# A two-layer attention and FFN kernel: the order of all engines, planned at build time before, written out as a table after

## The chip, the core and the metric

The kernel runs on one core of a Trainium2 chip. The metric is the device time of one launch in microseconds (us), median of several runs. The engines are PE (TensorE, matrix products; its weight loads are shown apart, as PEld), DVE (VectorE), ACT (ScalarE), POOL (GpSimd) and SP (SyncE, which here only issues DMAs). Each engine works through its own queue in the order in which the program lists it, and waits on semaphores where an operand comes from another engine.

## The reference, cut to what matters

x is 2,048 rows of 512 values in bf16, cut into 4 segments of 512 rows. Two layers follow each other, each of them attention and then an FFN, both on normalised rows and both added to x.

```python
x = A_x
x = x + _A_ref(_layernorm(x), wq, wk, wv, wo, beta)
x = x + _B_ref(_layernorm(x), w_gate, w_up, w_down)
x = x + _A_ref(_layernorm(x), wq, wk, wv, wo, beta)   # the same weights again
x = x + _B_ref(_layernorm(x), w_gate, w_up, w_down)

# _A_ref, for segments s = 0..3, with 32 heads of 16 values
p = softmax(qs @ ks.T * scale + causal_mask)          # inside the segment
a_mem = (phi(qs) @ M) / (phi(qs) @ z + 1e-06)         # phi(t) = t + 1 if t > 0 else exp(t)
o = g * a_mem + (1 - g) * (p @ vs)                    # g = sigmoid(beta), one per head
M = M + phi(ks).T @ vs ; z = z + phi(ks).sum()        # memory for the later segments
# _B_ref, with 1,792 hidden values
return (gelu(x @ w_gate) * (x @ w_up)) @ w_down
```

## The kernel before, in words

**Pieces of work.** The work is 8 pairs of an attention part and an FFN part, k = 0 to 7: layer k // 4, segment k % 4. An FFN part needs its own attention part, and an attention part of the second layer needs the FFN part of the same segment in the first. So the FFN of one segment can run beside the attention of the next ones, and nearly all of the span does so.

**Attention part k** (class `Att`, L799). Normalised rows `xn` (L734) are turned to `xnT`, by a DMA issued on SP (L577) or by PE with an identity matrix (L425). PE makes q, k and v by dense products of 128 x 512 (four of them, one per 128 rows of the weight, add up in one PSUM bank). The results are copied out of PSUM by DVE (L601) or ACT (L602), whichever the planner picks. `kx` is a masked copy of k (L546, L551). The scores are made in 72 rounds of 256 columns, two rounds to a visit (`score`, L1670): each visit is a run of small products with row tiles (32 or 16 rows, four tiles side by side) into four PSUM banks. ACT exponentiates two banks at a time, 1,024 values per row, or all four at once, 2,048 (L1710), into `pt`; POOL or DVE masks it (L1646, L1651, L1656). Value products (a "flush", `flush_item`, L1165) multiply `pt` with the values (`vaug`, `vz`, and `gel_sb` for k = 0) in column tiles: 128 rows by 32 columns, four side by side. DVE turns and scales the result (`byq` L1209, `ab` L1225, `aT` L1232). The memory part has small products (`mblk`, `zcols`, `phik`), with phi made by ACT (`e`, L966), a clipping on DVE or POOL (L989) and a sum on DVE (L970).

**FFN part k** (class `Ffn`, L1278). It adds the attention's output to x (L1287), takes the moments (L684), normalises, and makes 14 gate products (`wg_sb`), a gelu on ACT (L1448, L1323, L1337), 14 up products (`wu_sb`) that DVE multiplies in (L1388), and four down products of 14 steps each (`wd_sb`), added to x by DVE (L1287) and written out by SP.

**Three ways of tiling PE.** Whole (128 x 128), row tiles (scores) and column tiles (values). A dense product can be made whole, or as four column tiles of 32 columns each: the same result, four weight loads and four matmuls in place of one each. `product` (L605) decides:

```python
if ck.mode == "columns" or ck.mode == "rows" and (any(it.kind == "flush" and it.near() for it in items)):
    ck.tiling("columns")
    for c in range(4):
        r = slice(32 * c, 32 * c + 32)
        multiply(out[r], lhsT=lhsT[:, r], rhs=rhs, start=start, stop=stop, tile_position=(0, 32 * c))
else:
    ck.tiling("whole")
    multiply(out, lhsT=lhsT, rhs=rhs, start=start, stop=stop)
```

So once column tiles are in use they stay until the next score visit.

**What sets the order.** `order` (L402) plays the kernel through while it is built. It holds a clock (`Clocks`) with a duration for each operation, a model of each engine's queue, of PSUM banks that come free (`pick`, L1626), of slots and DMAs, and some 130 numbers (`POLICY`, `CHANGES` by 20 us, `NUDGES`, `VISITS`) that say how urgent each kind of work is. Step by step it takes the next score visit, value product or dense product that its clock calls ready, and writes the instructions of all engines as its clock serves them. A dense product that has begun is mostly run to its end (unless a part of its input is still missing). Where its clock finds no work for PE it writes a dummy product of 128 columns on a tile of ones (`warm`), so that PE goes on:

```python
if streams:
    ps = Psum()
    ps.bank = bank
    product(ps()[:, 0:P], warm[:], wide[:, 0, :])
```

All of this happens at build time: the chip gets a fixed order for each engine. All matmuls are issued in a helper, so that they have line 421 in the profile, and transposes by PE line 425.

Of the kernel before, what the change touches and what calls it, by code (L numbers as in the profile page):

```python
# [48 lines left out]


def shared(*tiles):
    return [(b, BOTH, ki, P * ki, C, C * n) for n, (b, ki) in enumerate(tiles)]


def whole_block(b):
    rounds = []
    for par in range(2):
        rounds += [([(b, (par,), *piece) for piece in pieces], n) for pieces, n in zip(FULL, DIAG)]
        if not par:
            rounds.append((shared(*((b, ki) for ki in range(TPS))), None))  # L60
    return rounds, ((0, 0, SHARED + 1), (1, SHARED, ROUNDS))


def table(halved):

    rounds, units = [], []

    def add(got):
        rounds.extend(got)
        return range(len(rounds) - len(got), len(rounds))  # L70

    def early(b):
        return [([(b, (par,), *piece) for piece in EARLY], 2) for par in range(2)]

    def late(b):
        return [([(b, (par,), *piece) for piece in pieces], n) for pieces, n in LATE for par in range(2)]

    for b in range(1 if halved else KT):
        got, parts = whole_block(b)
        at = add(got)  # L80
        units.append((b, None, [((par,), [at[i] for i in range(i0, i1)]) for par, i0, i1 in parts]))
    if halved:
        a1, s12, a2 = add(early(1)), add([(shared((1, 0), (1, 1), (2, 0), (2, 1)), None)]), add(early(2))
        a3, s3 = add(early(3)), add([(shared(*((3, ki) for ki in range(TPS))), None)])
        units += [(1, 0, [(BOTH, [*a1, *s12])]), (2, 0, [(BOTH, [*a2, *s12])]), (3, 0, [(BOTH, [*a3, *s3])])]
        units.append((3, 1, [(BOTH, [*s3, *add(late(3))])]))
        l1 = add(late(1))
        s12 = add([(shared((1, 2), (1, 3), (2, 2), (2, 3)), None)])
        units += [(1, 1, [(BOTH, [*l1, *s12])]), (2, 1, [(BOTH, [*s12, *add(late(2))])])]
    assert len(rounds) == STEPS  # L90
    flushes = [(u, b, h, n, pars, used) for u, (b, h, fl) in enumerate(units) for n, (pars, used) in enumerate(fl)]
    return rounds, len(units), flushes


TABLES = [table(k in HALVED) for k in range(NK)]
FLUSHES = [[[f for f in TABLES[k][2] if max(f[5]) == t] for t in range(STEPS)] for k in range(NK)]
USERS = [[sum(t in f[5] for f in TABLES[k][2]) for t in range(STEPS)] for k in range(NK)]
UNIT0 = [sum(TABLES[i][1] for i in range(k)) for k in range(NK)]
FLUSH0 = [sum(len(TABLES[i][2]) for i in range(k)) for k in range(NK)]


BY_PE = {("xnTf", 0), ("xnTf", 1), ("xnTf", NK - 1)}
QUICK = {("xnTf", k): (2,) for k in HALVED}
# [11 lines left out]
POLICY = dict(
    flush_wait=-12.009, piece_slack=-25.599, kb_slack=-71.296, mem_slack=-20.591, qk_due=-62.012, e_q=-288.808,
    e_k=138.109, exp_slack=-4.686, e_slack=148.266, phi_slack=52.68, gelu_slack=19.624, act_evict=2.071,
    first_evict=4.769, gate_step=1.835, up_due=3.98, up_step=-6.05, down_due=84.578, down_step=14.696, upd_due=9.144,  # L120
    kb_act=663.078, vz_slack=0.687, x_dve=-0.049, v0_due=-232.366, x1_at=-21.812, x2_at=-35.702, x3_at=1.468,
    x3_load=-242.902, direct=2, gelu_tiles=0, look=-61.488, lag=0, wv_at=-9.865, xn_pool=-26.108, kb_pool=62.128,
    cut_pool=0.028, at_pool=-27.695, gate_due=4.711, shun=77.466, col_gap=6.814, hold=34, early=435.185,
    starve=-5.581, near=-26.359, cap=6, soon=-134.054, drain=-0.14, join=0, held=10, urge_a1=-29.527, urge_a2=-0.64,
    urge_a3=-0.468, urge_a4=-5.519, urge_a5=-268.031, urge_a6=-6.935, urge_a7=-34.222, urge_f0=-37.767,
    urge_f1=-6.779, urge_f2=-11.706, urge_f3=-0.081, urge_f4=51.11, urge_f5=-14.712, urge_f6=-5.12, urge_f7=-38.117,
    half_a1=14, half_a4=21, half_a5=4, half_a6=18, half_a7=14, half_f0=21, half_f1=8, half_f2=10, half_f3=24,
    half_f4=46, half_f5=6, half_f6=8, pair_a1=10, pair_a2=3, pair_a3=12, pair_a4=11, pair_a5=0, pair_a6=65,
    pair_a7=28, pair_f0=9, pair_f1=19, pair_f2=43, pair_f3=2, pair_f4=22, pair_f5=23, pair_f6=28, pair_f7=11,
    turn_a1=14, turn_a2=12, turn_a3=8, turn_a4=8, turn_a5=6, turn_a6=16, turn_a7=42, turn_f2=18, turn_f3=4,  # L130
    turn_f4=16, turn_f5=2, turn_f6=6)

# [1723 lines left out]
```

## Time and profile before

| what | before |
|---|---|
| median of 3 runs (lowest, highest) | 539.28 us (539.02, 539.95) |
| the profiled execution, its span | 539.06 us (the page gives 539.1) |
| instructions | 20,839 |
| matmul records, weight loads on PE | 9,006, 9,072 |
| HBM read, written | 9.70 MB, 2.10 MB |
| granted PE clock, all 40 slices | 9 (90% or more) |

The profiled execution is one run of the same program, 0.2 us under the median; one core, so that its span is its time. The page gives busy time of each engine and its share of the span. A row of a group reads: line, engine, operation, out<-in, shapes, count | busy time and mean duration in ns | idle time of the engine just before, and what ended it. A row of the timeline reads: start and length in us, engine, line, operation, count, and in brackets the idle time before. A matmul's recorded end is modelled, and consecutive matmuls overlap in the records, so that durations of single matmuls add up to more than PE's time; the distance of their starts is what PE needs. A row of waits reads: who waited for whom, us in total, times, longest.

### The profile page before, as it was taken

To read this page: it belongs to the slowest core of one execution; us is meant where nothing else is said; L and a number is where in the kernel's file an instruction comes from. 1 tells how busy PE (TensorE), PEld (TensorE's weight loads), DVE (VectorE), ACT (ScalarE), POOL (GpSimd) and SP (SyncE) were. 2 spreads that over 40 slices of the span, in tenths; PEclk is the share of its full clock that TensorE was granted. 3 is DMA by queue.
4 is the path that set the end of the run, shared out by engine and by line. 5 is a ranking of instruction groups with operands and counts; after the bars stand their busy time and mean duration, and the time that the engine had idled before them with its cause. 6 is when DMAs were issued, how large, how long until landed. Compare 5 with 4: busy or idle time off the path is not lost.

```text
span 539.1 us, 20839 instructions
## 1 busy us (share of the span) xinstructions
PE 521.3 (97%) x9006; PEld 274.5 (51%) x9072; DVE 449.0 (83%) x849; ACT 433.2 (80%) x559; POOL 286.2 (53%) x360
## 2 busy tenths in 40 slices
PE   8999999999999999999999999999989999999997
PEld 4444467446654454554544454454554456555444
DVE  7998897899999997898997999878988786786342
ACT  6999997998999978999899778889789968830320
POOL 4997853279778656647572387550655253301000
PEclk9999999999999999999999999999999999999999
DMA  8349302422011123311432120310121004100001
GB/s 270 85 109 208 93 19 54 128 41 62 13 32 41 24 46 49 52 33 21 52 80 32 23 43 12 71 35 9 33 71 24 0 16 98 14 2 30 11 0 40
DMA packets 69134, 27.96 MB, mean 52 GB/s; under 512 B 53426, under 2 KB 69042, under 8 KB 69042
## 3 DMA queue, kind: packets, MB, share of 16 engines
q1 hardware_dynamic: 68752, 26.36, 22.1%
q8 instruction: 71, 1.16, 0.9%
q10 hardware_dynamic: 290, 0.26, 0.1%
q14 instruction: 21, 0.17, 0.1%
HBM read 9.70 MB, written 2.10 MB: 22 GB/s over the span
## 4 chain that ended last, share of the span: by engine, by line
PE 77%; DVE 11%; DMA 4%; issue 3%; POOL 3%; ACT 2%; DVEq 0%; POOLq 0%; ACTq 0%
PE ps L421 76%; DVE st L684 2%; DVE x_sb L1287 2%; ACT pt L1710 2%; DVE xn L734 2%; DMA xnT<-xn 2%; DMA amT<-am 2%; DVE byq L1209 1%; DVE ab L1225 1%; POOL pt L1646 1%; PE ps L425 1%; DVE phiq L970 1%; POOL rs L721 0%; DMA x_sb<-in_A_x_dram 0%; POOL pt L1651 0%
## 5 line engine op out<-in xcount | busy, mean ns | idle before, releaser
L1710 ACT ACTIVATE pt<-ps 128x1024 bf16<-128x1024 f32 (+1 forms) x274 | 277.8, 1072 | 39.5 <-PE ps L421 34.4
L1646 POOL TENSOR_SCALAR_AFFINE_SELECT pt<-pt 128x256 bf16<-128x256 bf16 (+1 forms) x192 | 108.2, 577 | 143.1 <-ACT pt L1710 138.3
L421 PE MATMUL ps<-xnT,wg_sb 128*32 128x512 bf16 (+3 forms) x940 | 106.5, 362 | 1.4 <-issue 1.1
L421 PE MATMUL ps<-wd_sb,gel_sb 128*32 128x512 bf16 (+3 forms) x879 | 102.8, 364 | 2.9 <-issue 1.9
L421 PE MATMUL ps<-xnT,wu_sb 128*32 128x512 bf16 (+1 forms) x816 | 99.6, 379 | 0.6 <-issue 0.2
L1388 DVE TENSOR_TENSOR gel_sb<-gel_sb,ps 128x512 bf16<-128x512 bf16 x112 | 74.4, 682 | 23.6 <-PE ps L421 22.1
L421 PEld LDWEIGHTS <-gel_sb 128*32 128x32 bf16 (+1 forms) x1086 | 50.7, 97 | 45.1 <-issue 4.8
L421 PEld LDWEIGHTS <-wu_sb 128*32 128x32 bf16 (+1 forms) x826 | 44.4, 97 | 50.2 <-issue 0.6
L421 PEld LDWEIGHTS <-wg_sb 128*32 128x32 bf16 (+1 forms) x954 | 46.9, 97 | 38.3 <-issue 2.0
L1287 DVE TENSOR_TENSOR x_sb<-x_sb,ps 128x512 bf16<-128x512 bf16 (+1 forms) x68 | 43.1, 642 | 20.5 <-PE ps L421 20.2
L1209 DVE STREAM_TRANSPOSE byq<-ps 128x512 f32<-128x512 f32 x64 | 45.2, 709 | 14.6 <-PE ps L421 13.4
L989 POOL TENSOR_SCALAR e<-e 128x512 bf16<-128x512 bf16 x31 | 49.8, 1608 | 3.8 <-ACT e L966 3.1
L1651 POOL TENSOR_SCALAR_AFFINE_SELECT pt<-pt 64x1024 bf16<-64x1024 bf16 x34 | 39.4, 1158 | 14.7 <-ACT pt L1710 10.0
L1448 ACT ACTIVATE gel_sb<-gel_sb 128x512 bf16<-128x512 bf16 (+1 forms) x81 | 45.9, 652 | 0.1
L684 DVE BATCH_NORM_STATS2 st<-x_sb 128x6 f32<-128x512 bf16 x60 | 40.8, 679 | 0.3
L601 DVE CAST gel_sb<-ps 128x512 bf16<-128x512 f32 x48 | 32.3, 680 | 7.9 <-PE ps L421 7.4
L421 PE MATMUL ps<-pt,vaug 128*32 128x256 bf16 (+2 forms) x1344 | 35.4, 239 | 0.2 <-POOL pt L1646 0.2
L421 PE MATMUL ps<-xnT,wk_sb 128*32 128x512 bf16 (+3 forms) x238 | 33.8, 353 | 0.5 <-issue 0.3
L421 PE MATMUL ps<-xnT,wq_sb 128*128 128x512 bf16 (+3 forms) x205 | 32.3, 347 | 2.0 <-DMA xnT<-xn 0.9
L421 PEld LDWEIGHTS <-vaug 128*32 128x32 bf16 x1344 | 26.7, 97 | 11.6 <-issue 4.2
L421 PE MATMUL ps<-q,kx 32*128 32x64 bf16 (+2 forms) x1120 | 30.8, 217 | 0.8 <-DVE x_sb L1287 0.8
L421 PE MATMUL ps<-wv_sb,xnT 128*32 128x512 bf16 (+1 forms) x194 | 30.6, 380 | 1.1 <-issue 0.6
(116 smaller groups left out, 704.4 us busy)
## 6 DMA issues: line engine op xcount, KB each, us to landing
vz<-vaug SPq DMA_DIRECT2D x14, 136.0 KB, 2.9
wg_sb<-in_B_w_gate_dram SPq DMA_DIRECT2D x8, 224.0 KB, 4.0
wu_sb<-in_B_w_up_dram SPq DMA_DIRECT2D x8, 224.0 KB, 4.4
wd_sb<-in_B_w_down_dram SPq DMA_DIRECT2D x7, 256.0 KB, 3.5
x_sb<-in_A_x_dram SPq DMA_DIRECT2D x3, 512.0 KB, 6.6
out_dram<-x_sb SPq DMA_DIRECT2D x12, 128.0 KB, 1.8
xnT<-xn SPq DMA_TRANSPOSE x48, 2.4
wk_sb<-in_A_wk_dram SPq DMA_DIRECT2D x2, 256.0 KB, 4.2
```

The costliest lines, as they stand in the source:

```text
L421: nc.tensor.matmul(*args, **named)
L601: ck.dve.post(ck.made(), slack + pol.drain, (0.673, lambda: nc.vector.tensor_copy(out=dst(), in_=src()), end), taken=taken)
L684: nc.vector.bn_stats(out=self.st6[:, 0, :], in_=x_sb[:, self.tt0 + j, :])
L734: eng.tensor_scalar(out=xn[:], in0=x_sb[:, self.tt0 + j, :], scalar1=self.mv[:, j, 1:2] if self.quick else self.mv[:, j, 0:1], scalar2=sel ...
L989: lambda eng: eng.tensor_scalar(out=e[0][:], in0=e[0][:], scalar1=1.0, scalar2=None, op0=ALU.min), summed)
L1209: nc.vector.transpose(out=(self.byq[:, pars[0], :, :].rearrange("p a c -> p (a c)") if h is None else self.byq[:].rearrange("p u a c -> p ...
L1287: ck.dve.post(ck.made(), slack, (0.15 + 0.00104 * (c1 - c0), lambda: nc.vector.tensor_tensor(out=xt, in0=xt, in1=ps()[:, 0:c1 - c0], op=AL ...
L1388: ck.dve.post(ck.made(), pol.drain, (0.683, lambda: nc.vector.tensor_tensor(out=g, in0=g, in1=ps()[:], op=ALU.mult), lambda t: (ps.read(t) ...
L1448: return (0.205 + 0.427 * (f1 - f0), lambda: nc.scalar.activation(out=g, in_=g, func=ACT.Gelu_apprx_tanh), lambda t: self.gelu_done(t, f0, ...
L1646: nc.gpsimd.affine_select(out=view, in_=view, pattern=[[0, 4], [0, n], [1, C]], compare_op=ALU.is_ge, fill=0.0, base=C, channel_multiplier=-1)
L1651: nc.gpsimd.affine_select(out=view, in_=view, pattern=[[0, 4 * TPS], [1, C]], compare_op=ALU.is_ge, fill=0.0, base=0, channel_multiplier=-1)
L1710: nc.scalar.activation(out=pt_all[:, slots[0]:slots[0] + 2, 2 * p:2 * p + 2 * n, :].rearrange("p r h c -> p h r c"), in_=ps_all[:, b0:b0 + ...
```

## The change

The planner goes. In its place stands a table, `ORDER`, of 2,559 entries, in which each entry is one step of one engine: its code, then its numbers. `Q/1/0/0/4/0/1` is four steps of the q product of part 1, block 0, into bank 0, as column tiles (last number 1); `S/0/0/4/6/0` is a score visit of part 0 into the banks from 4 and from 6 and slot 0; `e` and `E` are exponentials of two and of four banks; `F` is a value product; `W`, `G`, `P`, `O` are down, gate, up and output products; `l` and `L` are gelus; `M` masks; `Zu`, `Zg`, `Zo`, `Zd` load weights, `X` a segment of x. `run` reads the entries and calls a function for each. The bank, the tiling, the engine and the place are thus given per entry, and a dense product may be cut into pieces of 1, 2 or 3 steps with other work between them. The table has no dummy products. The operations themselves are the same, down to their shapes; only the start of the program (to the first score visit) has its old order.

Counted in the two built programs, before and after: 9,072 and 10,757 matmuls on PE. Dense products of 512 columns: 1,235 and 786 whole, 1,924 and 3,720 instructions of column form (four to a product). Changes of tiling on PE: 319 before, 365 after. Exponentials of two banks: 260 to 146, of four banks: 14 to 71. Transposes by PE: 64 to 48, by DMA (rows): 48 to 52. Clippings on DVE 17 to 31 and on POOL 31 to 17; normalisations on DVE 57 to 44 and on POOL 7 to 20. Evictions move between ACT and DVE by a few. SP issues the weights of the FFN in other places, some of them ahead of the first turned rows. The moments have a place of their own for each part (`mv`, `rs`), where before two parts shared one.

```diff
-class Clocks:
-    MM = {512: 0.2158, 128: 0.056}
-    SWITCH = 0.109
...
-def order(pol, nc, cst, seg, wrk, psp, A_x, A_wq, A_wk, A_wv, A_wo, A_beta, B_x, B_w_gate, B_w_up, B_w_down, out):
-    ck = Clocks()
...
-    while streams or items or opened or held or ck.busy():
...
-        if rounds_now():
-            score()
-            continue
...
-            if streams:
-                ps = Psum()
-                ps.bank = bank
-                product(ps()[:, 0:P], warm[:], wide[:, 0, :])
...
+ORDER = """
+Zu/3 Zo/3 Zu/2 X/3 m/g/0/0 x/1/0/0/0 Zg/3 c/0 S/0/0/4/6/0 Q/0/2/0/1/0/1 e/0/0/0 Q/0/1/0/4/1/0 st/1/0 e/0/0/1
...
+""".split()
+def run(nc, cst, seg, wrk, psp, A_x, A_wq, A_wk, A_wv, A_wo, A_beta, B_x, B_w_gate, B_w_up, B_w_down, out):
...
+    def product(dst, lhsT, rhs, columns, start=True, stop=True):
+        if columns:
+            for c in range(4):
+                r = slice(32 * c, 32 * c + 32)
+                multiply(dst[r], lhsT=lhsT[:, r], rhs=rhs, start=start, stop=stop, tile_position=(0, 32 * c))
+        else:
+            multiply(dst, lhsT=lhsT, rhs=rhs, start=start, stop=stop)
...
+    def dense(code, k, b, h, n, bk, columns):
+        name = (code, k, b, h)
+        if name not in done:
+            done[name], bank[name] = 0, bk
+        pairs, group = ops_of(code, k, b, h)
+        for _ in range(n):
+            i = done[name]
+            done[name] += 1
...
+            l, r = pairs[i]
+            product(dst, l(), r(), columns, i % size == 0, i % size == size - 1)
...
+    for token in ORDER:
+        code, *arg = token.split("/")
...
+        if code in ("Q", "K", "V", "O", "G", "P", "QH", "KH", "GH", "W"):
+            dense(code, *i)
+        elif code == "S":
+            score(*i)
+        elif code == "F":
+            values(*i)
...
+        elif code == "e":
+            exponential(k, b, i[2], 1)
+        elif code == "E":
+            exponential(k, b, 0, 2)
```

More of the change, by code (lines that the diff above doesn't have):

```diff
@@ L59, in whole_block @@
         if not par:
[L60 to L103, printed above, removed]
+            rounds.append(([(b, BOTH, ki, P * ki, C, C * ki) for ki in range(TPS)], None))
+    return rounds
+ROUNDS_OF = [r for b in range(KT) for r in rounds_of(b)]
+USED = [(0, SHARED + 1), (SHARED, ROUNDS)]
 BANKS = 8
@@ L605, in product @@
-    def product(out, lhsT, rhs, start=True, stop=True):
-        if ck.mode == "columns" or ck.mode == "rows" and (any(it.kind == "flush" and it.near() for it in items)):
-            ck.tiling("columns")
-            for c in range(4):
-                r = slice(32 * c, 32 * c + 32)
-                multiply(out[r], lhsT=lhsT[:, r], rhs=rhs, start=start, stop=stop, tile_position=(0, 32 * c))
-            ck.count += 4
-        else:
-            ck.tiling("whole")
-            ck.count += 1
-            multiply(out, lhsT=lhsT, rhs=rhs, start=start, stop=stop)
@@ L1481, in first_stats @@
+    xnT[0] = place(seg, [P, KT, L], "xnTa0", "xnT")
+    q[0], kf[0] = (wd_sb[:, KT * i:KT * (i + 1), :] for i in range(2))
+    kx[0] = kx0
+    st6 = [place(wrk, [P, 1, 6], "bnst", "st6", F32, 4) for _ in range(TPS - 1)]
     def first_stats(j):
@@ new lines, in run @@
+    first_product("k", ps_all[:, 0, 0:half], half, L)
+    nc.scalar.activation(out=kf[0][:, 0, half:L], in_=ps_all[:, 0, 0:half], func=ACT.Copy)
+    nc.vector.tensor_scalar(out=cden[:].rearrange("p (a h) -> p h a", a=2), in0=tmp_e.rearrange(
+        "p (h a) -> p h a", a=2), scalar1=1.0, scalar2=None, op0=ALU.add)
+    nc.vector.tensor_scalar(out=tmp_e2[:], in0=tmp_e2[:], scalar1=1.0, scalar2=None, op0=ALU.add)
+    bank, slot, done = {}, {}, {}
+    phiq, phik, zk, e_of, am_of, amT, aT, ab, byq, rdm, memory, xn_of = ({} for _ in range(12))
@@ new lines, in dens, with memory_product @@
+    def dens(k):
+        return ps("D", k)[:, 0:TPS * H].rearrange("p (j b h) -> p j b h", b=4, h=8)
+    def memory_product(code, k, b, n, bk, columns):
+        name = (code, k, b) if code == "N" else (code, k)
+        if name not in done:
+            done[name], bank[name] = 0, bk
+        for _ in range(n):
+            i = done[name]
+            done[name] += 1
+            if code == "N":
+                product(ps(*name)[:, i * P:(i + 1) * P], phiq[k][:, b, i * P:(i + 1) * P], memory[k - 1][0][:, b, :], columns)
+            elif code == "D":
+                j, c = i // 4, i % 4
+                product(dens(k)[:, j, c, :], phiq[k][:, c, j * P:(j + 1) * P], memory[k - 1][1][:, c, :], columns)
+            else:
+                j, b2 = i // 4, i % 4
+                for c in range(4):
+                    multiply(sums(k)[32 * c:32 * c + 32, b2, :], lhsT=phik[k][:, j, b2 * P + 32 * c:b2 * P + 32 * c + 32],
+                             rhs=by_head(vaug(k))[:, j, 4 * b2 + c, :, 0:DH], start=(i == 0), stop=(i == 15),
+                             tile_position=(0, 32 * c))
```

1833 lines of the change are left out of this document (581 added, 1252 removed).

## The prediction

> **What bounds the kernel now.** The page's busy times and chain come first: is one engine full, and does the end hang on it?
>
> ```profile
> PE 521.3 (97%) x9006; PEld 274.5 (51%) x9072; DVE 449.0 (83%) x849; ACT 433.2 (80%) x559; POOL 286.2 (53%) x360
> PE 77%; DVE 11%; DMA 4%; issue 3%; POOL 3%; ACT 2%; DVEq 0%; POOLq 0%; ACTq 0%
> ```
>
> PE is full and holds 77% of the chain. DVE's 11% says that the chain does leave PE now and then. Next the busy times by stretches of 20 us (in each row PE, PEld, DVE, ACT, POOL), to see where PE is not full and who is full beside it.
>
> ```profile
> 0.00:20.00 20.00, 17.43 (x137) 8.34 (x140) 15.65 (x47) 14.61 (x25) 12.32 (x27) 1.00 0.64 195
> 20.00:40.00 20.00, 19.02 (x306) 9.42 (x311) 19.52 (x46) 19.91 (x29) 19.59 (x24) 1.00 0.46 114
> 80.00:100.00 20.00, 18.89 (x434) 13.55 (x433) 16.29 (x32) 17.21 (x24) 7.41 (x11) 1.00 0.23 59
> 380.00:400.00 20.00, 17.85 (x327) 9.59 (x318) 19.42 (x34) 15.33 (x18) 13.78 (x19) 1.00 0.27 62
> 520.00:540.00 20.00, 15.90 (x87) 8.41 (x86) 5.27 (x9) 1.19 (x2) 0.00 (x0) 1.00 0.08 27
> sum 540.00, PE 521.25 PEld 274.52 DVE 449.01 ACT 433.18 POOL 286.23; mean PE 19.31 PEld 10.17 DVE 16.63 ACT 16.04 POOL 10.60
> ```
>
> Between 20 and 520 us PE is busy 521.25 - 17.43 - 15.90 = 487.9 of 500 us, so 12.1 us are open. Part of it is no waiting: the page counts 9,006 matmuls but 9,072 weight loads, so 66 records are lost. A recorded matmul of 512 columns lasts 0.380 us, while the next starts 0.216 us later (both rows are below, under PE's stream), so a lost one leaves a visible hole of 0.216 - 0.164 = 0.052 us: 3.4 us in all. About 8.6 us are waits. From 20 to 40 us ACT, DVE and POOL are as full as PE. PE's own waits, named:
>
> ```profile
> PE ps L421 <- issue: 6.8, 37, 1.1
> PE ps L421 <- DMA xnT<-xn: 1.1, 3, 0.6
> PE ps L421 <- DVE byq L1209: 1.0, 2, 0.8
> PE ps L421 <- DVE x_sb L1287: 0.8, 1, 0.8
> ```
>
> The first holds the lost records and one wait for code (below); the second is normalised rows that a DMA turns; the last two are PSUM banks that DVE had not yet emptied. So nothing but PE's own work (streaming plus changes of tiling) and these 8.6 us can shrink.
>
> **PE's stream.** The changed order has the same products. Counted along the two orders, it drops 39 dummy products of 128 columns (19 whole, 20 column tiles, four of which run side by side: 24 in time) and 16 of the 64 transposes. Prices:
>
> ```profile
> L421 PE MATMUL ps<-xnT,wu_sb 128*128 128x512 bf16 x312 | 71.3, 380 | 0.6 <-issue 0.2
> 492.58 1.00 PE ps L425 x16
> 506.40 1.89 PE L421 MATMUL ps<-xnT,wg_sb 128*128 128x512 bf16 x8
> 508.12 1.89 PE L421 MATMUL ps<-xnT,wu_sb 128*128 128x512 bf16 x8
> 469.95 1.04 PE L421 MATMUL ps<-xnT,wg_sb 128*32 128x512 bf16 x16
> 470.82 5.56 PE L421 MATMUL ps<-xnT,wu_sb 128*32 128x512 bf16 x97
> ```
>
> Sixteen products of 128 columns take 1.00 us, 0.06 each: 16 + 24 of them are -2.4 us. Whole: eight in 508.12 - 506.40 = 1.72, 0.216 each. As column tiles: 16 instructions, four groups, in 0.87, 0.217 a group. So the 449 products of 512 columns that turn from whole into four column tiles cost nothing while their loads stay hidden, and another product may follow at once, so single pieces of several products may alternate.
>
> A rule of the Trainium skill speaks against that ("TensorEngine Tiling (Array Packing)", Restrictions and Gotchas): column tiling excludes the fast weight load. The loads' own row is
>
> ```profile
> L421 PEld LDWEIGHTS <-wu_sb 128*32 128x32 bf16 (+1 forms) x826 | 44.4, 97 | 50.2 <-issue 0.6
> ```
>
> If four loads of 0.097 stood in line in front of a group, it would take 0.39 us and not 0.217, and 449 groups would add 77 us. The rows at 469.95 show them hidden; I keep that as a rival.
>
> **Changes of tiling.** Counted along the order there are 319 before and 365 now (363 after the start): 36 from column to whole tiles for 4, 39 back for 25, the rest around the 144 visits of score products, as before. The price, in PE's timeline:
>
> ```profile
> 222.62 1.46 PE L421 MATMUL ps<-xnT,wg_sb 128*128 128x512 bf16 x6
> 224.01 0.63 PE L421 MATMUL ps<-pt,vaug 128*32 128x256 bf16 x24
> 224.46 0.29 PE L421 MATMUL ps<-pt,vz 128*32 128x64 bf16 x16
> 224.69 0.40 PE L421 MATMUL ps<-q,kx 32*128 32x256 bf16 x12
> 225.02 0.40 PE L421 MATMUL ps<-mblk,phiq 128*128 128x128 bf16 x4
> ```
>
> Six whole products are 1.30 us, yet 1.39 pass to the column tiles. These stream 1,280 columns (0.54 us at 0.216 for 512), yet 0.68 pass to the scores; those stream 512 (0.216), yet 0.33 pass. Each change leaves 0.09 to 0.14, some of it small groups' own cost; 0.104 is my value. 46 more are +4.8 us (4.1 to 6.4). The skill's rule (same page, Key Properties) is that a change of mode drains the engine; the rows agree at 0.1 us. Where these changes stand matters: 31 of the 46 fall into the first 80 us of PE's work, where the 20 to 40 us row has three other engines full. Here is PE there, ahead of the products of segment 1, before:
>
> ```order
> L421 LDWEIGHTS wd_sb
> L421 MATMUL ps<-wd_sb 128x256
> L421 LDWEIGHTS warm
> L421 MATMUL ps<-warm 128x128
> L421 LDWEIGHTS warm
> L421 MATMUL ps<-warm 128x128
> L421 LDWEIGHTS warm
> L421 MATMUL ps<-warm 128x128
> L421 LDWEIGHTS xnT
> L421 MATMUL ps<-wv_sb,xnT 128x512
> ```
>
> and in the changed order at about the same place (wd_sb is still storage of segment 0's q and k here):
>
> ```order
> L485 LDWEIGHTS wk_sb
> L485 MATMUL ps<-xnT,wk_sb 128x512
> L483 LDWEIGHTS wk_sb
> L483 MATMUL ps<-xnT,wk_sb 32x512
> L483 LDWEIGHTS wk_sb
> L483 MATMUL ps<-xnT,wk_sb 32x512
> L483 LDWEIGHTS wk_sb
> L483 MATMUL ps<-xnT,wk_sb 32x512
> L483 LDWEIGHTS wk_sb
> L483 MATMUL ps<-xnT,wk_sb 32x512
> ```
>
> The dummies went, and in their place one product changes tiling half way. If PE would wait there anyway, it is free; I still charge it, because PE's work is what is sure.
>
> **Code.** PE's instructions come in pieces of 256.
>
> ```profile
> q8 instruction: 71, 1.16, 0.9%
> 85.45 0.28 PE L421 MATMUL ps<-pt,vz 128*32 128x64 bf16 x13
> 86.79 0.21 PE L421 MATMUL ps<-pt,vz 128*32 128x64 bf16 x3 [1.06 <-issue]
> ```
>
> 18,144 instructions are 71 pieces; 21,514 will be 84. The wait at 86.79 ends where the 2,744th instruction stands, after the quickest 290 instructions of the program: 2.4 us by the prices above. In the changed order the quickest 290 ahead of such a place take 4.25 us, so this wait should go (-1.1) and none come, although there are 13 more pieces.
>
> **ACT.** Two exponentials of two banks become one of four in 57 more cases (71 for 14):
>
> ```profile
> L1710 ACT ACTIVATE pt<-ps 128x1024 bf16<-128x1024 f32 x260 | 251.6, 1029 | 34.5 <-PE ps L421 29.7 <-POOL pt L1646 3.3 <-issue 0.5
> L1710 ACT ACTIVATE pt<-ps 128x2048 bf16<-128x2048 f32 x14 | 26.2, 1875 | 5.0 <-PE ps L421 4.7 <-issue 0.2
> ```
>
> 57 x (2 x 1.029 - 1.875) = 10.4 us less on ACT. ACT's queue, from the first score on, before:
>
> ```order
> L1710 ACTIVATE pt<-ps 128x2x2x256 x4
> L602 ACTIVATE wd_sb<-ps 128x512 x2
> L602 ACTIVATE gel_sb<-ps 128x16x2x16
> L1710 ACTIVATE pt<-ps 128x2x2x256 x2
> L602 ACTIVATE gel_sb<-ps 128x16x2x16 x2
> L1710 ACTIVATE pt<-ps 128x2x2x256 x2
> ```
>
> and now:
>
> ```order
> L657 ACTIVATE e<-wd_sb 128x512
> L600 ACTIVATE pt<-ps 128x2x2x256 x2
> L492 ACTIVATE wd_sb<-ps 128x512 x2
> L600 ACTIVATE pt<-ps 128x4x2x256
> L657 ACTIVATE e<-wd_sb 128x512
> L492 ACTIVATE wd_sb<-ps 128x512
> L600 ACTIVATE pt<-ps 128x2x2x256
> L492 ACTIVATE gel_sb<-ps 128x16x2x16
> ```
>
> Pairs became fours, and the exponentials e for the memory sums came ahead of the scores' own. Off the path this is worth nothing in itself; it loosens the stretch in which ACT was full. The price: the first two banks of a four come free 0.85 us later (1.875 - 1.029). DVE takes 14 clippings from POOL and gives it 13 normalisations:
>
> ```profile
> L734 DVE TENSOR_SCALAR xn<-x_sb,mv,rs 128x512 bf16<-128x512 bf16 x57 | 28.7, 540 | 2.6 <-POOL rs L721 1.6 <-DMA phik<-e 0.5 <-DMA amT<-am 0.3
> L989 DVE TENSOR_SCALAR e<-e 128x512 bf16<-128x512 bf16 x17 | 6.5, 390 | 0.6 <-ACT e L966 0.4
> ```
>
> 14 x 0.39 - 13 x 0.54 = -1.6 us, so DVE stays as full as it was.
>
> **Loads.** SP now issues 0.8 MB more (three pieces of wu and wg, one of wo) ahead of the first turned rows.
>
> ```profile
> 10.00:12.00 2.00, 1.67 (x22) 0.84 (x26) 1.92 (x10) 1.76 (x3) 1.46 (x2) 1.00 1.10 356
> 14.00:16.00 2.00, 2.00 (x28) 0.85 (x28) 1.79 (x5) 2.00 (x5) 1.45 (x3) 1.00 0.03 8
> 17.10 5.21 SPq L577 DMA_TRANSPOSE xnT<-xn  x4
> ```
>
> At 356 GB/s they take 2.3 us; the queues are empty from 14 us, the turns start at 17.10. Hidden; without that cover it is at most 2.3 us at segment 1.
>
> **Banks.** Along the order with the prices above I took how much PE work stands between a bank's last product and its next. Returns under 1.1 us: 3 of 490 before, 35 of 487 now; under 1.3: 29 and 58. What a return needs, from the end of the program:
>
> ```profile
> 532.73 3.22 PE L421 MATMUL ps<-wd_sb,gel_sb 128*128 128x256 bf16 x28
> 532.93 0.69 DVE L1287 TENSOR_TENSOR x_sb<-x_sb,ps 128x512 bf16<-128x512 bf16 x1 [2.34 <-PE ps L421]
> 535.99 0.42 DVE L1287 TENSOR_TENSOR x_sb<-x_sb,ps 128x256 bf16<-128x256 bf16 x1 [1.11 <-PE ps L421]
> ```
>
> 28 products of half 0.216 end at 535.75; DVE starts at 535.99; 0.24 + 0.69 = 0.93 us with DVE idle. So the shortest, 0.86 (five, some with smaller copies), have nothing to spare, and those near 1.1 no room for a DVE that is late. Before, bank waits came to 1.8 us (byq, x_sb) for 29 returns under 1.3, 0.06 each: 58 give 3.6. Ends: 0, and 32 more returns at 0.35, half of a DVE instruction in front, 11 us.
>
> **The sum.** Against this execution's 539.06 us (the median, 539.28, is 0.2 above): stream -2.4, changes of tiling +4.8, waits 8.6 down to 4.6. Those 4.6 are: code 0, banks 2.7 (between 1.8 and 3.6, since fewer DVE copies stand behind two short exponentials), turned rows 1.1 as before, and 0.8 of the other 4.7, the small gaps of which most stand in the first 80 us, where ACT is relieved. That is 539.06 - 2.4 + 4.8 - 4.0 = 537.5, or 537.7 as a median. Ends: all waits gone, 533.1; banks at their upper end, 11 for the 2.7, 546.0.
>
> **The rivals.**
> 1. Slower. DVE becomes the pacemaker through the banks: a return of about 1 us makes PE wait whenever DVE is one instruction late, and the changes of tiling stay paid. For: 35 returns for 3, DVE at 19.5 of 20 us in 20 to 40 and 380 to 400, and the wait of 0.84 for x_sb stood at a return of 1.0. Against: each such wait gives DVE time. At half of the upper end, 6.4 for the 2.7, the time is 541.4. It decides once waits exceed 6.2 us.
> 2. No change. The code wait goes, the other waits stay as they are: 8.6 - 1.1 = 7.5 gives 540.6; with a quarter of the small gaps gone too, 539.4. For: the last 80 us of dense work have next to no waits to give, and in the first 80 us other engines set the pace.
> 3. The column groups' loads show: +77, 616. The rows at 469.95 exclude it wherever full groups follow each other. This is what the skill's rule on the fast load would mean here.
>
> **How the numbers follow.** What a measurement of this kernel can tell from no change is about 0.2%, 1.1 us. Forecast 537.7, chance 0.49 that it is faster by more than that; no change 0.21; slower by banks 0.29; loads 0.01. That is faster 0.49, same 0.21, slower 0.30. The range reaches from nearly all waits gone, 533.6, to 543.3, two thirds of the way to the upper end of the banks. The likeliest case's own range is 533.6 to 538.
>
> **What would show it.** In the changed profile: PE's stretches from 460 us on as full as before; no wait of 1 us on issue; whole-to-column changes at 0.1 us; column groups at 0.217; ACT busy about 423 us. Right: PE waits of 4 to 5 us between 20 and 520. Wrong: waits for DVE at banks of 6 us and more, or changes that cost more than 0.11, or waits for turned rows at segment 1 beyond 2 us.

## The result, and the profile after

| | before | after |
|---|---|---|
| median (lowest, highest) | 539.36 us (539.02, 539.95), 4 runs | 544.70 us (543.52, 545.90), 4 runs |
| ratio of after to before | | 1.0097, 95% interval 1.0080 to 1.0115 |
| the profiled execution: its span, its time | 539.06 us, not shown | 543.5 us, 545.27 us |
| the same kernel again, in a later measurement | 539.23 us (15 runs) | 543.22 us (542.31 to 544.09, 5 runs), ratio 1.0073 (1.0060 to 1.0087) |

The changed kernel is slower by 4 to 5 us; the forecast of 537.7 was wrong in sign, and its range ended at 543.3.

One thing comes ahead of the rows. The text before the prediction took the profiled execution's span for its time. Every run shown since has both, and the time is 1.7 to 1.8 us longer than the span: 545.27 for 543.5, and 540.43 for 538.7 in a second look at the kernel before. So the execution on which the sum stood had a time of some 540.8 us, 1.4 above its kernel's median and not 0.2 below it.

The page of the changed kernel, its busy times and the instruction queue:

```profile
PE 523.0 (96%) x10692; PEld 280.8 (52%) x10757; DVE 444.0 (82%) x859; ACT 426.1 (78%) x496; POOL 284.7 (52%) x360
q8 instruction: 84, 1.38, 1.1%
```

PE is busy for 1.7 us more (though 65 matmul records are lost in this trace and 66 in that of the kernel before), DVE and ACT for less, and the code has its 84 pieces. Next the busy times by stretches of 20 us, in each row PE, PEld, DVE, ACT, POOL:

```profile
180.00:200.00 20.00, 18.50 (x354) 9.45 (x346) 17.55 (x35) 16.21 (x16) 11.24 (x18) 1.00 0.16 33
340.00:360.00 20.00, 18.35 (x425) 10.01 (x424) 15.86 (x30) 15.38 (x17) 8.94 (x14) 1.00 0.34 50
380.00:400.00 20.00, 18.59 (x499) 10.13 (x493) 15.62 (x29) 15.98 (x15) 10.17 (x16) 1.00 0.19 36
420.00:440.00 20.00, 18.78 (x216) 8.85 (x222) 15.70 (x27) 17.32 (x23) 5.82 (x8) 1.00 0.00 1
500.00:520.00 20.00, 18.84 (x396) 11.29 (x392) 7.15 (x12) 6.75 (x12) 0.00 (x0) 1.00 0.04 12
```

In these five, PE is open for 1.2 to 1.7 us while no other engine is full: ACT stands at 7 to 17 of 20 us. (In the first four rows 0.2 to 0.5 us of it are mostly holes left by lost records; each row also has a single wait of 0.8 to 1.2 us.) So it isn't a shortage of some engine's time; single things come late. PE's waits by name:

```profile
PE ps L485 <- issue: 6.0, 38, 0.2
PE ps L595 <- ACT pt L600: 3.8, 6, 1.1
PE ps L483 <- issue: 1.4, 2, 1.2
PE ps L483 <- ACT pt L600: 1.3, 2, 1.1
PE ps L483 <- ACT vaug L492: 0.6, 1, 0.6
```

The first is the lost records, and two of the six waits in the second row (0.26 us each, at 45.2 and 56.6 us) stand where a record is lost too; a trace of the same early order with all its records (e3) has neither. No row names DVE at a bank, the rival that had been feared. The waits name ACT's exponentials (L600), which hold the PSUM banks that the next score visit writes to, and one of 1.2 us names nothing.

How much such holes hide shows a second profile of the kernel before (e1 below). It has all 9,072 matmul records, and its page and its wait on issue read:

```profile
PE 528.6 (98%) x9072; PEld 274.3 (51%) x9072; DVE 449.9 (84%) x849; ACT 433.3 (80%) x559; POOL 286.6 (53%) x360
PE ps L421 <- issue: 1.1, 2, 1.0
```

Its span is 0.4 us shorter, yet PE is busy for 7.3 us more. Between 20 and 520 us, 4.7 us are open, where the first trace has 12.1. Of the 37 waits on issue one is left, that for code, beside one of 0.1 us; the other 36 (5.7 us, 0.16 each) were holes. All lost records are whole products of 512 columns, and where such a product stands next to a change of tiling its hole is mostly 0.16 us, not 0.052. The two traces of the changed kernel lack the same 65 products.

The largest waits of the changed kernel, in order of time (PE and ACT around 178 us, then PE alone):

```profile
177.90 0.40 PE L595 MATMUL ps<-q,kf 16*128 16x256 bf16 x12
178.39 1.28 ACT L600 ACT_TABLE_LOAD   x1 [2.02 <-PE ps L595]
179.68 1.88 ACT L600 ACTIVATE pt<-ps 128x2048 bf16<-128x2048 f32 x1
181.61 0.40 PE L595 MATMUL ps<-q,kf 16*128 16x256 bf16 x12 [1.13 <-ACT pt L600]
...
348.57 1.48 PE L483 MATMUL ps<-xnT,wq_sb 128*32 128x512 bf16 x24 [1.13 <-ACT pt L600]
399.21 0.40 PE L595 MATMUL ps<-q,kx 32*128 32x64 bf16 x10 [1.09 <-ACT pt L600]
435.70 0.29 PE L595 MATMUL ps<-q,kx 32*128 32x64 bf16 x7 [0.78 <-ACT pt L600]
502.25 1.05 PE L483 MATMUL ps<-xnT,wu_sb 128*32 128x512 bf16 x16 [1.16 <-issue]
```

The first four rows are one event. PE ends its scores at 178.3. ACT had idled for 2.02 us, and only when the scores are there does it change its function table from gelu to exponential, 1.28 us, and then exponentiate, 1.88 us. PE's next score visit uses the same banks. They come free at 181.56 us, 3.3 us behind the end of the first visit; PE was through with the work between at 180.48 and waits for 1.13 us. At 435.7 it is the same again, with a load at 432.47. The two kernels have as many table loads, 14 each; how those ahead of exponentials stand differs. Before, and after (count | busy, mean | idle time of ACT just ahead):

```profile
L1710 ACT ACT_TABLE_LOAD x6 | 7.7, 1283 | 0.1
```

```profile
L600 ACT ACT_TABLE_LOAD x5 | 6.4, 1283 | 6.8 <-PE ps L595 4.2 <-DVE gel_sb L821 2.5
```

Before, ACT never idled ahead of one: there were exponentials left over from earlier visits for it to go on with (the last visit had begun 7 to 9 us before each of these six loads). In the table that replaced the planner they were already done, and the load stands between the scores and PE. The Trainium skill ("ScalarE: Activation LUTs", Step-by-step: what each stage is for) says that the load is placed right before the activation that needs it; the rows agree on the place, with 1.28 us from the load to the exponential, where the Trainium skill has about 2.7 with the drain.

**Counted from the starts of PE's matmuls** along the two orders (products at their streaming price, each change of tiling at the distance that its kind leaves, 0.096 to 0.112 us, and the rest waits), the profiled executions differ so: stream -2.1, changes of tiling 32.8 to 37.8, waits 12.6 to 14.3 (start of the program included). Together +4.6, where the spans differ by 4.4. The forecast had -2.4, +4.8 and -4.0. Waits counted in this way include small delays that the overlapping records hide; as open time in the rows, without holes, the waits of 0.18 us and more between 20 and 520 us are 4.5 us before and 6.8 after.

### The profile page after: what moved, and what is told of

It is laid out like the page before. It is cut to its first block, busy times and chain, and to the rows that moved or that the text cites. A ratio compares the mean times of both kernels' runs of the same rounds, so it can differ in the third digit from the quotient of the medians.

```text
span 543.5 us, 23981 instructions
## 1 busy us (share of the span) xinstructions
PE 523.0 (96%) x10692; PEld 280.8 (52%) x10757; DVE 444.0 (82%) x859; ACT 426.1 (78%) x496; POOL 284.7 (52%) x360
## 5 line engine op out<-in xcount | busy, mean ns | idle before, releaser
L600 ACT ACTIVATE pt<-ps 128x1024 bf16<-128x1024 f32 (+1 forms) x217 | 274.2, 1302 | 46.7 <-PE ps L595 36.7
L483 PE MATMUL ps<-wd_sb,gel_sb 128*32 128x512 bf16 (+1 forms) x1300 | 70.2, 356 | 0.0
L483 PE MATMUL ps<-xnT,wu_sb 128*32 128x512 bf16 x1060 | 66.4, 380 | 1.2 <-issue 1.2
L483 PE MATMUL ps<-xnT,wg_sb 128*32 128x512 bf16 (+1 forms) x1000 | 60.7, 361 | 0.0
L485 PE MATMUL ps<-xnT,wg_sb 128*128 128x512 bf16 (+1 forms) x236 | 52.9, 349 | 1.6 <-issue 1.1
L755 ACT ACTIVATE gel_sb<-gel_sb 128x512 bf16<-128x512 bf16 x86 | 48.1, 623 | 5.6 <-DVE gel_sb L494 5.3
L483 PEld LDWEIGHTS <-gel_sb 128*32 128x32 bf16 x1300 | 33.2, 97 | 26.2 <-issue 3.0
L393 POOL TENSOR_SCALAR xn<-x_sb,mv,rs 128x512 bf16<-128x512 bf16 x20 | 44.3, 2215 | 1.7 <-DVE phiq L665 0.8
L485 PE MATMUL ps<-xnT,wu_sb 128*128 128x512 bf16 x172 | 41.9, 379 | 1.6 <-issue 1.3
L483 PEld LDWEIGHTS <-wu_sb 128*32 128x32 bf16 x1060 | 28.4, 97 | 26.9 <-issue 3.6
L485 PE MATMUL ps<-wd_sb,gel_sb 128*128 128x512 bf16 (+1 forms) x167 | 36.8, 355 | 1.7 <-issue 1.3
L483 PEld LDWEIGHTS <-wg_sb 128*32 128x32 bf16 x1000 | 25.6, 96 | 18.5 <-issue 1.8
L485 PEld LDWEIGHTS <-wg_sb 128*128 128x128 bf16 x254 | 22.6, 98 | 21.9 <-issue 3.2
```

Of the source, the lines that this page charges most:

```text
L393: eng.tensor_scalar(out=xn[:], in0=x_sb[:, tile_of(m) + j, :], scalar1=mv[:, m, j, 0:1], scalar2=rs[:, m, j, :], op0=ALU.subtract, op1=ALU ...
L483: multiply(dst[r], lhsT=lhsT[:, r], rhs=rhs, start=start, stop=stop, tile_position=(0, 32 * c))
L485: multiply(dst, lhsT=lhsT, rhs=rhs, start=start, stop=stop)
L600: nc.scalar.activation(out=pt_all[:, s:s + 2, 2 * p:2 * p + 2 * n, :].rearrange("p r h c -> p h r c"), in_=ps_all[:, b0:b0 + 2 * n, :].rea ...
L755: nc.scalar.activation(out=dst, in_=src, func=ACT.Gelu_apprx_tanh)
```

## The experiments

Each is compared with runs of the kernel before on the same chip. The changed kernel's own two measurements lie 5.3 and 4.0 us above those, so differences under about 1 us aren't read between measurements. The lines of helpers move by a few between these kernels (L478 and L480, L479 and L481, L482 and L484 are the column and whole matmuls that stand at L483 and L485 in the changed kernel).

| run | median (lowest to highest) | before beside it | ratio, 95% |
|---|---|---|---|
| e1 before, again | 540.43, one run | 539.54 | |
| e2 fewest changes | 539.68 (538.06 to 540.65) | 539.54 | 1.0000 (0.9988 to 1.0011) |
| e3 table early | 540.70 (539.47 to 541.45) | 539.54 | 1.0023 (1.0013 to 1.0034) |
| e4 fewest, early, moves | 537.00 (536.49 to 537.58) | 539.54 | 0.9956 (0.9944 to 0.9969) |
| e5 no fours | 544.89 (543.70 to 546.29) | 539.17 | 1.0111 (1.0095 to 1.0127) |
| e6 shifted code | 541.38 (540.54 to 542.79) | 539.17 | 1.0046 (1.0033 to 1.0059) |
| e7 late changes only | 539.35 (537.88 to 539.53) | 539.17 | 0.9993 (0.9981 to 1.0004) |
| e8 changes in the tail | 547.30 (546.98 to 548.22) | 539.17 | 1.0157 (1.0144 to 1.0170) |
| e9 before, no dummies | 539.86 (538.28 to 540.68) | 539.23 | 1.0010 (1.0000 to 1.0019) |
| e10 changed, again | 543.22 (542.31 to 544.09) | 539.23 | 1.0073 (1.0060 to 1.0087) |
| e11 early changes only | 541.12 (540.39 to 542.13) | 539.23 | 1.0035 (1.0023 to 1.0048) |
| e12 whole tail | 537.28 (536.41 to 537.67) | 539.23 | 0.9963 (0.9949 to 0.9976) |

**The two kernels again.** No edit.

> The kernel before, unchanged, looked at once more, to see how far PE's waits differ from one execution to the next. If the waits belong to the program, PE's busy time in each stretch of 20 us and the places of the waits repeat, and the span is within 1 us of 539.06. If they depend on chance (which packet stands behind which), single waits of about 1 us come and go, and the span moves by 1 to 2 us with them.

> The changed kernel, unchanged, timed and looked at once more beside the others. If its waits belong to its order, those for exponentials at 181.6 and 435.7 us and behind the table loads come back at the same score visits; those for turned rows at 348.6, 399.2 and 502.3 us come back as long as the code is fetched at the same places; single waits in the first 65 us may come and go, 1.4 us in all. Time 544 to 546.

The kernel before repeats its waits: the one for code stands at 86.77 (0.97 us, 1.06 the first time), that at 399.8 again; smaller ones change. The changed kernel repeats its own at the same products: 181 us 1.13, 348 us 1.19, 398 us 0.88, 501 us 1.04 by the timeline. So these belong to the order and the code. What comes and goes is the first 65 us: by the first visit of part 1 the two executions of the changed kernel are 0.8 us apart, and with four other runs of the same early order 1.4 us.

**Fewest changes of tiling.** 156 last numbers of dense and memory entries were set so that between two score visits all are column tiles (where a value product stands there) or all whole:

```diff
-K/0/3/0/1/7/1 S/0/2/3/5/4 xn/v/1/3/4 q/s/0/2 K/0/3/0/1/7/1 ... V/0/1/0/4/1/0
+K/0/3/0/1/7/0 S/0/2/3/5/4 xn/v/1/3/4 q/s/0/2 K/0/3/0/1/7/0 ... V/0/1/0/4/1/0
```

> The changed kernel with its order of all engines untouched, and only the last number (whole or column tiles) set so that PE changes tiling as seldom as the order allows: 291 times for 365. Theory (changes of tiling lie on the path at 0.104 us each): 74 x 0.104 = 7.7 us less, 544.7 down to about 537. Rival (many changes stand where PE would wait for another engine anyway, so that a wait takes their place): no more than half of it, 541 or above.

It lies between the two: level with the kernel before, so 4 to 5 us less for 74 changes, 0.05 to 0.07 each by the medians. By the starts the changes fell by 7.8 us and 3.1 us came back as waits, so part of the changes stood where PE waits anyway. But the edit also adds 72 matmuls, so that the code behind lies elsewhere, and two of the late turns described under "Turned rows and code", those at 348 and 502 us, are gone in its trace. Up to 300 us, ahead of them, 69 of the 74 changes are gone, and this execution has gained 1.5 and 2.2 us on the two of the changed kernel: 0.02 to 0.03 each. The next three runs show where a change costs its price.

> As the run with fewest changes and moves, but with the changed kernel's own tiling up to 93 us (visit 12 of part 1), so that 46 of the 74 changes of tiling come back there. If changes in that stretch stand where PE waits for ACT, DVE and POOL anyway, the time stays at 537.0 (within 0.7). If each lies on the path at 0.104 us, 541.8. By the run with fewest changes alone, which had gained 1.5 us by 93 us, 0.033 each: 538.5.

> The changed kernel with the fewest changes of tiling up to 93 us (visit 12 of part 1) and its own tiling from there: 46 changes fewer, all in the stretch in which ACT, DVE and POOL are as full as PE. On the path: 4.8 us less. Free: the time of the changed kernel within 0.7. By the difference of the two runs with the moves (539.35 and 537.0), half: 2.2 less.

> The changed kernel with 20 pieces of dense products after the last score visit turned from column tiles to whole, one at a time between others: 40 changes of tiling more, in a stretch where PE alone sets the pace, and nothing else changed. At 0.104 us each it is 4.2 us slower, 548.9. If a change costs more than 0.11 with other products around it, above 549.1. If the prediction's price is too high, below 547.5.

The edits are the same kind, up to or from entry `S/1/12/1/6/0`, and for the tail 20 such:

```diff
-O/7/3/0/3/1/1 ... P/6/1/0/3/6/1
+O/7/3/0/3/1/0 ... P/6/1/0/3/6/0
```

By the medians, 46 changes fewer in the first 93 us gained 2.1 us (543.22 to 541.12, measured side by side), and put back into the kernel with the moves they cost 2.4 us (537.00 to 539.35; 2.7 with each against the kernel before beside it). The traces say that most of this isn't the changes. PE begins score visit 12 of part 1, up to which these edits reach, at (us; e5 also has its fours split there, and e4, e7 and e12 one eviction moved):

```
the changed kernel's own early tiling   after 93.33, e10 92.58, e3 92.27, e5 93.11, e7 92.07, e8 91.95   mean 92.55
fewest changes up to there              e2 91.81, e4 92.11, e11 91.59, e12 91.96                         mean 91.87
```

That is 0.7 us for 46 changes, 0.015 each, and single executions scatter by more. e7 and e4 are level there; e7's span is 1.6 us longer at the end, and its trace has waits of 0.9 us at 138 and 0.3 at 452 and 496, all at products on turned rows, where e4 waits less. e11 is 1.0 us ahead of e10 there and 2.9 at the end; it gained the rest where the turns at 348, 399 and 502 are no longer late. So the early changes, in a stretch where ACT and DVE are busy for 17 to 19 of 20 us, are almost free.

In the tail, 40 more cost 2.6 to 4.1 us by the medians. In the trace the part behind the last score visit is 3.4 us longer than in e10, although the late turn at 502 us (1.0 us) is gone: 4.4 us, 0.11 each. The timeline there shows the price bare:

```profile
477.75 0.61 PE L480 MATMUL ps<-xnT,wu_sb 128*128 128x512 bf16 x2
478.28 0.62 PE L478 MATMUL ps<-xnT,wu_sb 128*32 128x512 bf16 x8
478.83 0.60 PE L480 MATMUL ps<-xnT,wu_sb 128*128 128x512 bf16 x2
479.36 0.40 PE L478 MATMUL ps<-wo_sb,aT 128*32 128x512 bf16 x4
479.70 0.60 PE L480 MATMUL ps<-xnT,wu_sb 128*128 128x512 bf16 x2
```

Two whole products (0.43 us) take 0.53 to the next row, two column groups 0.55, one group (0.22) 0.34: 0.10 to 0.12 a change.

**The table loads.**

```diff
+        elif code == "ex":
+            nc.scalar.activation(out=early[:], in_=masks[:, 0:1], func=ACT.Exp)
...
-p/5/9 l/5/3 P/5/10/0/4/1/0
+p/5/9 l/5/3 ex/0 P/5/10/0/4/1/0
```

> The changed kernel with six exponentials of one column added on ACT, each right behind the last gelu ahead of an exponential, so that ACT changes its function table there and not when the scores are ready. Theory (four-bank exponentials come late because 1.28 us of table loading stand between scores and exponential, at 178 and 432 us, where ACT had idled 2.0 and 1.5 us before): the waits of PE at 181.6 (1.2 us) and 435.7 (1.0 us) go, 544.7 down to 542.5. Rival (ACT is late for its load as a whole): the waits move to the next score visit, and the time stays within 0.7 us of 544.7.

The theory held, and the gain is larger than forecast: 540.70. The same place in this kernel's timeline (ACT, then PE):

```profile
175.01 1.28 ACT L801 ACT_TABLE_LOAD   x1
176.30 0.20 ACT L801 ACTIVATE early<-masks 128x1 f32<-128x1 f32 x1
177.02 1.88 ACT L596 ACTIVATE pt<-ps 128x2048 bf16<-128x2048 f32 x1 [0.52 <-issue]
```

```profile
176.52 0.40 PE L591 MATMUL ps<-q,kf 16*128 16x256 bf16 x12
...
179.04 0.40 PE L591 MATMUL ps<-q,kf 16*128 16x256 bf16 x12
```

The load now runs while PE is still at other work, the exponential starts right behind the scores, and PE's next visit waits for nothing. The waits at 181 and 435 went, and a third of 0.3 us at 108.8: 2.5 us. The median fell by 4.0 against the first measurement of the changed kernel and, each taken against the kernel before beside it, by 2.8 against the second; what is above 2.5 isn't explained by a row.

**Fours of banks.**

```diff
-E/0/1
+e/0/1/0 e/0/1/1
```

> The changed kernel with all 71 exponentials of four banks split into two of two banks each, in the same places of ACT's queue: 71 x (2 x 1.029 - 1.875) = 13 us more work on ACT, while the first two banks come free 0.85 us earlier. If the late return of the first banks is what PE waits for (the price named in the prediction and set at nothing), the time falls by the 3.8 us of waits for exponentials, to about 541. If the fours were right and ACT is what lacks time, it rises above 546. If neither matters, within 1 us of 544.7.

Neither: 544.89, which is 0.4 to 1.7 us above the changed kernel's two measurements, each taken against the kernel before beside it. The waits stay where they were (181.2, 398.5, 435.1 us), 0.1 to 0.3 us shorter. So the 0.85 us by which the first two banks come free earlier hardly matters. About ACT the run says less than was meant: its exponentials are busy for 278.4 us against 274.7, so 3.7 us of work were added and not 13. Two exponentials of 1,024 that follow each other start 0.92 us apart, though each record lasts 1.02, and behind one of 2,048 the next starts 1.77 us later; a four saves 0.07 us, not 0.18.

**Turned rows and code.** The waits at 348.6, 399.2 and 502.3 have another cause. The instructions waiting at 348.57 and 502.25 wait for the DMAs that turn `xnT`; a turn counts as landed when 16 parts are there. The trace's records of landings, of the one piece of code being fetched at that time, and PE:

```
15 parts landed by   the last   fetch of a piece of code   PE (or ACT) goes on
346.62               348.49     346.09, for 1.32           348.57
395.25               397.08     394.74, for 1.26           ACT 397.10, PE 399.21
500.33               502.16     499.83, for 1.25           502.25
```

Each time one of the 16 parts comes 1.8 us after the others, and a 16 KB piece of code was fetched meanwhile. In this trace 31 transfers have a last part that is over 0.4 us late; with 27 of them a fetch was under way in the 2.6 us before. That alone says little, since the same holds for a little over half of all transfers; but it holds for every one whose last part is over 1.5 us late. At 399 the chain has one step more: on ACT an exponential for the memory sums (`x/0/7/1/3`) waits for the turn and stands ahead of the exponential whose banks PE needs:

```profile
393.63 1.88 ACT L600 ACTIVATE pt<-ps 128x2048 bf16<-128x2048 f32 x1
397.10 1.15 ACT L657 ACTIVATE e<-q 128x512 bf16<-128x512 bf16 x2 [1.59 <-DMA xnT<-xn]
398.15 3.69 ACT L600 ACTIVATE pt<-ps 128x1024 bf16<-128x1024 f32 x3
```

To see whether the fetch is the cause, the code was moved and the order left:

```diff
-    for _ in range(WARM):
+    for _ in range(WARM - 4):
...
+    for i in range(100):
+        r = slice(32 * (i % 4), 32 * (i % 4) + 32)
+        multiply(ps_all[r, 0, 0:8], lhsT=warm[:, r], rhs=warm[:, 0:8], start=True, stop=True, tile_position=(0, r.start))
```

> The kernel with the early table loads, and ahead of everything 100 dummy column products of 8 columns in place of four of the twelve dummy products with which PE starts: every later instruction of PE stands 192 places later in its pieces of 256, so that each piece is fetched earlier beside the rest of the work. Theory (the turned rows at 345, 395 and 497 us come 1.8 us late on one of 16 landings because a fetch of code is under way on it): the waits of 1.1, 1.3 and 1.0 us at those places go, 540.7 down to about 538, unless a fetch now meets another transfer that PE waits for. Rival (the order is short of time there): the three waits stay, and the time is 540.7 to 541.5.

In the trace the three waits are gone, and no part of these three turns is late; the products stand without a gap:

```profile
345.83 0.82 PE L482 MATMUL ps<-xnT,wg_sb 128*32 128x512 bf16 x12
346.48 1.47 PE L482 MATMUL ps<-xnT,wq_sb 128*32 128x512 bf16 x24
...
495.69 1.60 PE L482 MATMUL ps<-wd_sb,gel_sb 128*32 128x512 bf16 x40
497.11 1.05 PE L482 MATMUL ps<-xnT,wu_sb 128*32 128x512 bf16 x16
```

With fewer early changes (e11) the code of the later part lies elsewhere too, with the entries the same, and those three waits went there as well (one of 1.0 us came at 466); where it lies as it did (e3, e5, e10) they came back. But the time didn't fall: 541.38, 0.7 above the run that it was made from. Score visit by score visit, its trace gains 1.1, 1.3 and 0.5 us on that run's trace where the three waits were. It loses as much elsewhere: 1.0 us by 93 us, 0.8 of it ahead of the first score visit, behind the new dummies, and then new waits of 0.6 us at 129, 0.4 at 216 and 0.7 at 465. So the cause of the three waits is shown, and so is what their removal gives in place; that the whole gains by it is not.

**Moves.**

```diff
-x/0/7/1/3 M/g/6/21 S/6/11/2/4/8 f/6/3 x/0/7/0/2 ... e/6/11/0
+M/g/6/21 S/6/11/2/4/8 f/6/3 ... e/6/11/0 x/0/7/1/3 x/0/7/0/2
...
-P/7/9/0/4/2/1 w/6/1/0 w/6/0/0 W/6/3/1/3/0/1 W/6/3/2/9/6/1
+w/6/1/0 w/6/0/0 W/6/3/1/3/0/1 W/6/3/2/9/6/1 P/7/9/0/4/2/1
```

> Both edits at once, and four moves of single entries at the other places where PE waits: the exponentials of part 6, visit 11 ahead of two memory exponentials on ACT that wait for a transfer, one value eviction on ACT earlier, one memory product ahead of a score visit, and five entries of down products ahead of the first product that needs part 7's turned rows. Theory (terms add, each wait has one cause of its own): 7.7 + 2.2 + 1.3 + 0.6 + 1.2 = 13 us less than 544.7, about 532, below the kernel before. Rival (other engines set the pace once PE is faster): above 537.

537.00: 7.7 of the 13 us. With e12, which is made from it, it is the only run that beats both kernels, by 0.44% on the kernel before. PE in three of the stretches shown above:

```profile
180.00:200.00 20.00, 20.00 (x387) 10.24 (x389) 17.67 (x37) 15.06 (x16) 12.50 (x19) 1.00 0.18 36
340.00:360.00 20.00, 20.00 (x507) 10.85 (x509) 16.81 (x34) 16.42 (x19) 8.95 (x13) 1.00 0.25 30
380.00:400.00 20.00, 19.69 (x429) 11.30 (x431) 16.05 (x32) 17.58 (x17) 13.62 (x17) 1.00 0.31 49
```

From 180 us on PE is all but full (1.0 us open up to 520). This trace has all its records, so up to 0.5 us of the difference to each row above is only the holes there. The missing part is in the first 150 us, where the changes were almost free and waits of 0.2 to 0.5 us stand: there other engines do set the pace, as the rival expected for the whole.

**Dummies.**

```diff
+                quiet.append(1)
                 product(ps()[:, 0:P], warm[:], wide[:, 0, :])
+                quiet.clear()
```

(`multiply` then issues nothing.)

> The kernel before with its order of all engines kept and only the 39 dummy products of 128 columns left out, which the changed kernel doesn't have either. If they stood on the path, as the prediction charged them (24 in time by 0.06 us), the time falls by 1.4 us. If they filled places where PE waits for another engine anyway, PE waits there instead and the time stays within 0.4 us of the kernel before.

No gain, rather 0.6 us the other way. Where the dummies stood PE now waits for ACT:

```profile
21.26 0.38 PE L424 MATMUL ps<-wd_sb 32*128 32x64 bf16 x9 [0.32 <-ACT gel_sb L605]
21.73 1.02 PE L424 MATMUL ps<-wv_sb,xnT 128*128 128x512 bf16 x4
23.62 0.82 PE L424 MATMUL ps<-xnT,wq_sb 128*128 128x512 bf16 x3 [0.86 <-ACT pt L1713]
...
87.56 0.26 PE L424 MATMUL ps<-q,kf 16*128 16x192 bf16 x2 [0.95 <-issue]
```

The last row is of use for another point: the wait for code, at 86.8 in the middle of value products before, is now in a score visit, with 1,360 matmul records ahead of it in this trace and in the first one of the kernel before. It belongs to the place in the code and not to the work that stands there.

**Columns or whole.** The 112 column entries behind the last value product were made whole.

> The run with fewest changes and moves, with all dense products behind the last value product whole instead of column tiles: one change of tiling more, and 960 matmuls and as many weight loads fewer, 7.5 pieces of code. If a column group costs what a whole product does and code only costs where a fetch meets a turn, 537.0 within 0.7. If the number of instructions itself costs, by the 84 pieces for 71 about 0.1 us each, 536.2 or less.

537.28: no difference. A column group costs what a whole product does, and 7.5 pieces of code fewer gain nothing where no turn is disturbed.

## Why the prediction was wrong, point by point

- **The stream, -2.4.** Counted rightly (-2.1 by the starts), but 1.4 of it, the dummies, was no gain where it was tried: in the kernel before they filled places where PE waits (e9). The step that failed is that dummies were taken off PE's path without asking what ends there last. No run takes the 16 transposes away alone.
- **Changes of tiling, +4.8.** Right in size by the starts (32.8 to 37.8 us), and paid in full where PE alone sets the pace, 0.10 to 0.12 each in the tail. But 31 of the 46 were charged in the first 80 us, 3.2 us, and there a change costs about 0.015. The remark that they may be free if PE waits there was right; charging them all the same brought the number nearer to the result, by luck.
- **Waits, 8.6 down to 4.6.** This step failed twice, and with it the sign. First, the 8.6 us were misread. The lost records were taken off with 0.052 us each, 3.4 in all; the second trace of the kernel before, which lost none, has 4.7 us open, so they had made 7.4. The 4.7 us of "small gaps", of which 3.9 were booked as gain, were mostly such holes. With 4.7 for 8.6 the same sum is 539.06 - 2.4 + 4.8 - 0.1 = 541.4, slower. Second, the waits didn't fall: by the starts they rose by 1.7 us, as open time from 4.5 to 6.8.
- **What the new waits are.** Three parts of the forecast held: the wait for code went and none came; no wait of PE names DVE at a bank; early loads stayed hidden. Two failed. Turned rows were kept at 1.1 us as before; three late turns made 3.4 us of it. And the banks were looked for among returns with less than 1.3 us of PE's work between, and priced by DVE's copies. The two that cost most (1.13 us at 181.6, 0.78 at 435.7) have 2.2 and 2.5 us of PE's work between and needed 3.3, since ACT loads a table and exponentiates four banks in that time. ACT was costed by its busy time and by the release of banks; its queue is in order, and what stood at its head waited: a table load that could only start when scores were there, and memory exponentials behind a turn.
- **ACT.** Busy 426.1 us for about 423: a four saves 0.07 us and not 0.18. It was said to be worth nothing in itself, and 3.7 us more of it (e5) cost little. The price that the text named, the first two banks 0.85 us later, is next to nothing too.
- **Column groups** at the price of whole products: right (e12), so the third rival is out. The loads show in no row, and the rule that the prediction took from the Trainium skill changes nothing here.
- **Rival 1** had the right sign, with a time 2 to 3 us too low, but by a mechanism that no row shows: DVE at the banks. Of the signs listed for a wrong forecast only one was touched (changes at 0.10 to 0.12 us, for over 0.11). Of those listed for a right one, three failed: the waits are 6.8 us and not 4 to 5, one of 1.16 us stands on issue at 502 us, and PE is busy for 18.84 of 20 us from 500 on, where it was 19.90.
- **Rival 2** said that other engines set the pace in the first 80 us. There it was right (e11, e4); its 540.6 is 3 to 4 us too low.
- **The base.** The profiled span was taken for the time. Of the 7.0 us between 537.7 and 544.7, 6.0 lie in the span (0.3 stream, 0.2 changes, the rest waits), 1.75 between span and time; against that stand 0.6 by which the profiled execution of the changed kernel lay above its median and 0.2 that was added for the base.

What stays open: why single executions differ by up to 1.4 us in the first 65 us, what the early table loads gained beyond 2.5 us, and why the moved code brought new waits at 129, 216 and 465 us.

## What to carry to other kernels

Where a fixed order feeds an engine in order, ask of each item at the head of its queue what it waits for and who stands behind it; busy time and release of buffers don't show it. A function table is best changed while its engine is idle, by a tiny activation put right behind the last one of the other kind: six of them took 2.5 us of waits away. A gain that consists of work left out counts only where nothing else ends last. Before open time is read as waits, count the records: a profile that lost some shows holes. And an edit that adds or takes away instructions moves all code behind it, so read a difference at the place of the edit and not from the whole time alone.

## What the runs showed of the hardware

- A piece of code of 16 KB, fetched in 0.9 to 1.6 us (once 1.9), can delay one of the 16 parts of a transfer beside it by 1.8 us, and the transfer counts as landed only then. The Trainium skill ("Runtime: NRT & Kernel Launch", Instruction fetch mechanics) says that code comes in blocks of 16 KiB and that the cost of crossing one is mostly hidden; 84 pieces and no wait of PE for code in the changed kernel agree, but the cost can come back through a transfer. More pieces don't mean more late parts: 31 transfers have one in the first trace of either kernel, with 71 pieces and with 84. What counts is whether PE waits for the transfer that is hit.
- A change of tiling costs 0.11 us where PE alone sets the pace (e8), and about 0.015 in the first 93 us, by the means of six and four executions that scatter by more, where other engines set it.
- Exponentials of 1,024 values that follow each other on ACT start 0.92 us apart, though each record lasts 1.02 us.
- A trace can lack matmul records: 66 of 9,072 in one of the kernel before, none in another. The lost ones made 7.4 us look like open time.
- The profile puts a wait down to what came last in its records: the one at 348.57 is named for ACT there, and the landing of a turn at 348.49 ended it.
- The time of a run is 1.7 to 1.8 us longer than its span, for both kernels and all edits.
